# The first batch reordered and mixed at full width, with q and k loaded in two pieces instead of four, in an attention and Fourier-mix kernel

## The chip, the cores and the metric

The kernel runs on one core of a Trainium2 chip. The metric is the device time of one execution in microseconds (us). TensorE multiplies matrices, VectorE, ScalarE and GpSimd work on elements, and SyncE issues most of the transfers. In the profile they are called PE, DVE, ACT, POOL and SP; PEld is TensorE's loading of weights.

## What is computed

Eight batches, 576 positions, 8 heads of 64 channels. Attention is done in chunks of 64 positions; its output, seen as 512 channels per position, goes through a Fourier mix, a normalization and a feed-forward block:

```python
# attention, per batch and head, 9 chunks of 64 positions
scores = (q_c @ k_c.T) / 8
attn   = softmax(scores)
x      = attn @ v_c                       # [8, 576, 512] once the heads are side by side
# Fourier mix and feed-forward
mixed  = real(fft(fft(x, axis=1), axis=2))
u      = x + mixed
un     = (u - mean(u)) / sqrt(var(u) + 1e-6)
out    = u + relu(un @ w_ch1) @ w_ch2     # w_ch1 [512, 2048], w_ch2 [2048, 512]
```

The weights come in as 64-bit floats and are turned into 32-bit ones on the chip, on VectorE and ScalarE together ("rounding").

## The kernel before

All work is laid out by hand in one order. A batch has four tiles of 128 positions: `LO` tiles hold positions from the front, `HI` tiles their mirror images from the back. Each two batches share a tile `RE` with the two middle chunks. That makes 36 tiles; 9 of them belong to the first two batches (`first[2]` is 9). The Fourier sums use the mirror symmetry: a pair `LO[i]`, `HI[i]` is first *folded* (sums and differences), then multiplied by cosine and sine tables along the positions (`z`), then along the channels (`mix`).

From the third batch on, q and k aren't transposed on TensorE but in 32 x 32 blocks on VectorE. For this each of q and k is loaded in runs of 224 elements that overlap (the same positions twice, the second time shifted by 32 channels), so that the transposed blocks of one head fill 64 partitions:

```python
    def load(n):                                   # tiles n >= first[2]
                (b0, c0), (b1, c1) = chunks(n)
                parts = [(0, 32, b0, min(c0, c1))] if b0 == b1 else [(0, 16, b0, c0), (16, 16, b1, c1)]
                for g in range(4):
                    e, x0 = g // 2, g % 2 * 32
                    for r0, rows, b, c in parts:
                        from_ = src[b, e:H:2, c * CH:c * CH + 4 * rows, :].rearrange("j (p t) d -> p j (t d)", t=4)
                        eng.dma_start(out=t[32 * g + r0:32 * g + r0 + rows, :, 0:4 * D - 32],
                                      in_=from_[:, :, x0:x0 + 4 * D - 32])
    def att_S(n):                                  # scores of one tile: 16 products, 64 x 64 x 64
        for j in range(NJ):
            for e in range(2):
                for c in range(2):
                    r0, t0 = e * D, c * CH
                    nc.tensor.matmul(out=sc[t0:t0 + CH, e, j * CH:(j + 1) * CH],
                                     lhsT=a[r0:r0 + D, 2 * j + c, 0:CH], rhs=b[r0:r0 + D, 2 * j + c, 0:CH],
                                     start=True, stop=True)
        ...                                        # DVE: mx (maximum), ex (difference); ACT: exp
```

The first batch has nothing to hide behind, and runs ahead of all else: its attention, its folds, its mix, its normalization. `keep_warm` issues products whose result nobody reads.

```python
    def shift_early(i):                            # one row of each LO tile moves to the next tile
        if i == 0:
            nc.gpsimd.tensor_copy(...)             # three rows
        else:
            nc.scalar.copy(...)                    # three rows
    def fold(b, i):
        eng = nc.vector if b < 2 and (b, i) != (0, NM) else nc.gpsimd
        ...                                        # sum, two, two, pm, pm
    def fourier(b):
        for pair in range(2):                      # z: products of the folded tiles with the position tables
            ...
        def mixed(i):                              # half of the channels: 129 + 128 + 256 + 128 columns
            ...
            nc.scalar.copy(y[:, 0:HM + 1], mix[:, 0:HM + 1])
            nc.scalar.copy(y[:, DM:DM + 1], mix[:, 0:1])
        def both(y, mix):                          # the mirrored half of the channels from the sine part
            nc.vector.tensor_tensor(out=y[:, DM - 1:HM:-1], in0=y[:, 1:HM], in1=mix[:, HM + 1:DM], op=ALU.subtract)
            nc.vector.tensor_tensor(out=y[:, 1:HM], in0=y[:, 1:HM], in1=mix[:, HM + 1:DM], op=ALU.add)
        ...
        if b == 0:
            y, g = [mixed(i) for i in range(NM)], groups[0]
            for i in range(NM):
                ...                                # both, added, means, normed (un), turned (pt, unT), per tile
    ...
        for step, _ in enumerate(fourier(0)):
            for _ in range((2, 1, 0)[step]):
                round_next()                       # one 128 x 512 piece of a weight: 5 DVE and 3 ACT operations
```

After that TensorE runs the feed-forward block group by group: `up_first` and `down_plain` for the first batch, later forms (`up_halves`, `down_halves`) that save products with sums of weight blocks kept in HBM. `keep2` makes those sums of the second weight on VectorE, `keep1` those of the first on GpSimd. The attention and the mix of the next batch are laid in between, step by step (`t` counts the steps; the first group has 32, `begin[1]` is 32):

```python
                for _ in range(2 if n_w <= len(pieces) else 3):
                    if n_w > N_LAST + 2 and n_conv < 5 or n_w > len(pieces):
                        n_conv += 1
                        next(conv2, None)          # one operation of keep2
                if t == begin[1] - 1:
                    for _ in conv2:
                        pass
                if begin[1] <= t < begin[1] + KF // 2:
                    for _ in range(3):
                        next(conv1, None)          # one operation of keep1
```

Of the kernel before, what the change touches and what calls it, by code (L numbers as in the profile page):

```python
# [16 lines left out]
def kernel(  # L17
# [94 lines left out]

    LO, HI, RE = "lo", "hi", "rest"
    tiles, first = [], []
    for b in range(B):
        first.append(len(tiles))
        if b % 2 == 0:
            tiles.append((RE, b, 0))
        tiles += [(what, b, i) for what in (LO, HI) for i in range(NM)]
# [41 lines left out]
    dims = [start[:, d0 + o:d0 + o + n_] for o, n_ in ((0, HM + 1), (HM + 1, HM - 1), (2 * HM, HM + 1), (3 * HM + 1, HM - 1))]  # L161
# [3 lines left out]
    def load(n):  # L165

        for src, dst, nm, eng in ((q, qs, "q", nc.sync), (k, ks, "k", nc.scalar if n == 0 else nc.sync)):  # L170
            if n < first[1]:
                i = 2 * n + (nm == "k")
                t = start[:, (4 + i) * DM:(5 + i) * DM].rearrange("p (j r d) -> p j (r d)", r=2, d=D)
            else:
                t = one_p.tile([128, NJ, 4 * D], FP32, tag=nm, name=nm)
            if n >= first[2]:
                (b0, c0), (b1, c1) = chunks(n)
                parts = [(0, 32, b0, min(c0, c1))] if b0 == b1 else [(0, 16, b0, c0), (16, 16, b1, c1)]
                for g in range(4):
                    e, x0 = g // 2, g % 2 * 32  # L180
                    for r0, rows, b, c in parts:
                        from_ = src[b, e:H:2, c * CH:c * CH + 4 * rows, :].rearrange("j (p t) d -> p j (t d)", t=4)
                        eng.dma_start(
                            out=t[32 * g + r0:32 * g + r0 + rows, :, 0:4 * D - 32],
                            in_=from_[:, :, x0:x0 + 4 * D - 32],
                        )
                dst[n] = t
                continue
            t = t.rearrange("p j (r d) -> p (j r) d", d=D)[:, 0:H]
            (b0, c0), (b1, c1) = chunks(n)  # L190
            if b0 == b1 and c1 == c0 + 1:
                parts = [(0, 128, b0, c0)]
            else:
                parts = [(0, CH, b0, c0), (CH, CH, b1, c1)]
            for p0, np_, b, c in parts:
                eng.dma_start(
                    out=t[p0:p0 + np_], in_=src[b, :, c * CH:c * CH + np_, :].rearrange("h p d -> p h d")
                )
            dst[n] = t
# [15 lines left out]
    def load_tables():  # L215

        t = start[:, 0:(NM + 1) * 2 * NQ].rearrange("p (i r f) -> p i r f", i=NM + 1, r=2)  # L220
        for c in range(2 * NM):
            (i, r0), (j, p0) = divmod(c * CH, 128), divmod((NC - 1 - c) * CH, 128)
            nc.gpsimd.dma_start(out=t[r0:r0 + CH, i], in_=seq_tab[p0:p0 + CH, j])
        for r0 in (0, CH):
            nc.gpsimd.dma_start(out=t[r0:r0 + 1, NM], in_=seq_tab[0:1, 0])
            nc.gpsimd.dma_start(out=t[r0 + 1:r0 + CH, NM], in_=seq_tab[1:CH, NM])

    def load_dim_tables():
        nc.gpsimd.dma_start(out=dims[0], in_=dim_tab[:, 0, 0:HM + 1])
        nc.gpsimd.dma_start(out=dims[1], in_=dim_tab[:, 2, 1:HM])  # L230
        nc.gpsimd.dma_start(out=dims[2][0:1], in_=dim_tab[0:1, 1, 0:HM + 1])
        nc.gpsimd.dma_start(out=dims[3][0:1], in_=dim_tab[0:1, 3, 1:HM])

    def turn_tables():
# [5 lines left out]
        nc.gpsimd.tensor_copy(a[:, :, NL + 1:NQ], b[:, :, NL + 1:NQ])  # L240
        nc.gpsimd.memset(cx[:, 0:HQ + 1], 0.0)
        nc.gpsimd.tensor_copy(ce, dims[0][:, ::2])
        nc.gpsimd.tensor_copy(co, dims[0][:, 1::2])
        nc.gpsimd.tensor_copy(so, dims[1][:, ::2])
        nc.gpsimd.tensor_copy(so[0:1], dims[3][0:1, ::2])
        nc.gpsimd.tensor_copy(cx[:, HQ + 1:HM], dims[1][:, 1::2])
        nc.gpsimd.memset(cx[0:1, HQ + 1:HM], 0.0)
        nc.gpsimd.tensor_copy(cx[0:1, 0:HQ + 1], dims[2][0:1, ::2])
# [58 lines left out]
    def att_T(n):  # L307
# [4 lines left out]
        if n >= first[2]:  # L312
            for src, dst, nm in ((qs, qT, "qT"), (ks, kT, "kT")):
                a = src.pop(n).rearrange("p j (t b d) -> p j t b d", t=4, b=2)[:, :, :, 0]
# [3 lines left out]
                if kind(n) == HI:  # L318
                    to = to[:, :, ::-1]
                nc.vector.transpose(out=to.rearrange("p j c (r t) -> p j t c r", t=4), in_=a)  # L320
                if low:
                    nc.gpsimd.tensor_copy(t[:, :, :, 0:1], t[:, :, :, CH:CH + 1])
                dst[n] = t.rearrange("p j c t -> p (j c) t")
# [8 lines left out]
        if low and n == at[LO, 0, 1]:  # L332
            nc.scalar.copy(t[:, :, 0:1], t[:, :, CH:CH + 1])
        elif low:
            nc.gpsimd.tensor_copy(t[:, :, 0:1], t[:, :, CH:CH + 1])
# [5 lines left out]
        kT[n] = t.rearrange("p j (c t) -> p (j c) t", c=2)  # L341
# [3 lines left out]
    def att_S(n):  # L345
        a, b = qT.pop(n), kT.pop(n)
        sc = ps_a.tile([128, 2, 512], FP32, tag="att", name="sc")
        for j in range(NJ):
            for e in range(2):
                for c in range(2):  # L350
# [4 lines left out]
                        rhs=b[r0:r0 + D, 2 * j + c, 0:CH],  # L355
# [28 lines left out]
    def att_V(n):  # L384
# [35 lines left out]
        if kind(n) == HI:  # L420
            nc.gpsimd.tensor_copy(x[:, 0:1], x[:, DM:DM + 1])
# [3 lines left out]
    def shift_early(i):  # L425

        lows = [xt(at[LO, 0, j])[:, 0:DM] for j in range(NM)]
        rest = xt(rests[0])[0:1, 0:DM]
        if i == 0:
            nc.gpsimd.tensor_copy(first_rest[CH:CH + 1, 0:DM], rest)  # L430
            nc.gpsimd.tensor_copy(rest, lows[0][0:1])
            nc.gpsimd.tensor_copy(lows[0][0:1], lows[0][CH:CH + 1])
        else:
            nc.scalar.copy(lows[0][CH:CH + 1], lows[1][0:1])
            nc.scalar.copy(lows[1][0:1], lows[1][CH:CH + 1])
            nc.scalar.copy(lows[1][CH:CH + 1], first_rest[CH:CH + 1, 0:DM])
# [15 lines left out]
    def fold(b, i):  # L452

        eng = nc.vector if b < 2 and (b, i) != (0, NM) else nc.gpsimd
        two = one_p.tile([128, 2 * (HM + 1)], FP32, tag="two", name="two")
        if i < NM:
# [3 lines left out]
            nc.gpsimd.memset(s[:, DM:DM + 1], 0.0)  # L460
# [27 lines left out]
    def attention_early():  # L488
# [3 lines left out]
        def ready(n):  # L492
            for i in range(NM):
                if n == at[LO, 0, i]:
                    shift_early(i)
                if n == at[HI, 0, i]:
                    fold(0, i)
            if n == at[LO, 0, 0]:
                fold(0, NM)
            if n + 3 > hi:  # L500
# [55 lines left out]

    def fourier(b):
# [11 lines left out]
        for pair in range(2):  # L569
            if b == 0 and pair == 1:  # L570
                z = early_xp[0]
            else:
                z = [ps_t.tile([128, 512], FP32, tag="pt", name="z") for _ in range(2)]
# [59 lines left out]
        def added(y, n):  # L633
            x, w = xt(n), DM + (kind(n) == HI)
            eng = nc.gpsimd if kind(n) == HI and b > 0 else nc.vector
            eng.tensor_tensor(out=x[:, 0:w], in0=y[:, 0:w], in1=x[:, 0:w], op=ALU.add)  # L636

        def means(ns):
            st = sm_p.tile([128, 2, 2], FP32, tag="st", bufs=6 + NP, name="st")
            rstd = sm_p.tile([128, 2], FP32, tag="rstd", bufs=6 + NP, name="rstd")  # L640
            for j, n in enumerate(ns):
                bst = sm_p.tile([128, 6], FP32, tag="bst", name="bst")
                nc.vector.bn_stats(bst, xt(n)[:, 0:DM])  # L643
                nc.vector.bn_aggr(st[:, j], bst)  # L644
                sts[n] = st[:, j, 0:1], rstd[:, j:j + 1]
            g = slice(0, len(ns))
            nc.scalar.activation(out=rstd[:, g], in_=st[:, g, 1], func=ACTF.Ln, bias=eps)
            nc.scalar.activation(out=rstd[:, g], in_=rstd[:, g], func=ACTF.Exp, scale=-0.5)

        if b == 0:  # L650
            y, g = [mixed(i) for i in range(NM)], groups[0]
            def turned_(s):
                keep_warm(2)
                turned(0, s)

            keep_warm(4)
            for i in range(NM):
                y_ = both(*y[i])
                if i > 0:
                    normed(0, 1)  # L660
                    turned_(1)
                added(y_, g[2 * i])
                means(g[2 * i:2 * i + 1])
                added(y_, g[2 * i + 1])
                normed(0, 2 * i)
                means(g[2 * i + 1:2 * i + 2])
                turned_(2 * i)
            normed(0, 3)
            turned_(3)
            yield  # L670
            return
        for i in ((NM,) if h == 1 else ()) + tuple(range(NM)):
# [5 lines left out]
            yield  # L678

# [305 lines left out]
    with tc.manual_schedule():  # L985
# [6 lines left out]
        for n in range(3):  # L992
            load(n)
            load_v(n)
        for n in range(3, first[1]):
            load(n)
        for n in range(3, first[1]):
            load_v(n)
# [18 lines left out]
        for step, _ in enumerate(attention_early()):  # L1017
            if step == 0:
                load_tables()
                load_dim_tables()  # L1020
# [3 lines left out]
        keep_warm(5)  # L1024
        for step, _ in enumerate(fourier(0)):
            for _ in range((2, 1, 0)[step]):
# [29 lines left out]
        for g in range(NG):  # L1056
            for _ in mlp(g):
# [17 lines left out]
                for _ in range(2 if n_w <= len(pieces) else 3):  # L1075
# [3 lines left out]
                if t == begin[1] - 1:  # L1079
                    for _ in conv2:  # L1080
                        pass
                if begin[1] <= t < begin[1] + KF // 2:
# [57 lines left out]
```

## Time and profile before

| | before |
|---|---|
| time, median of 3 runs | 1139.6 us (1138.49 to 1141.79) |
| span of the profiled run | 1140.0 us, mean granted TensorE clock 0.995 |
| first product of the feed-forward block | at 65.10 us |
| TensorE busy in the 65.10 us before it | 43.56 us |
| TensorE busy in the 1074.90 us after it | 1050.21 us |
| VectorE, ScalarE, GpSimd busy in the span | 599.2, 290.3, 274.3 us |
| HBM read and written | 166.96 MB, 24.12 MB |

A line of the timeline gives start, duration, engine, line of the kernel, operation, what is written from what, shape, and the number of records merged into it; in brackets stands the idle time of the engine before it and what ended that. TensorE takes each 32-bit product in two passes, so a product has two records; a transposition has one. A line of the waits gives the total in us, how many times, and the longest.

### The profile page before, as it was taken

The numbers are of one execution on the slowest core, as the hardware profiler recorded it, in microseconds if no ns is written. First come the engines' busy times: TensorE is split into PE (matmuls) and PEld (weight loads), VectorE is DVE, ScalarE is ACT, GpSimd is POOL, SyncE is SP. The second block draws the span as 40 slices with busy tenths as digits, with TensorE's granted clock in tenths as the row PEclk, the third lists the DMA queues.
The fourth block names the chain that finished last, engine by engine and source line by source line (L and its number), as shares of the span: only waits on it lengthen the run. The fifth ranks groups of instructions, "written<-read, shape, count | busy, mean of one in ns | idle before, by whom it ended". The sixth has DMA issues, their size and how long they took to land. (4 is left out here: it accounts for less than half of the span.)

```text
span 1140.0 us, 18688 instructions
## 1 busy us (share of the span) xinstructions
PE 1093.8 (96%) x7040; PEld 846.3 (74%) x7040; DVE 599.2 (53%) x1241; ACT 290.3 (25%) x711; POOL 274.3 (24%) x406
## 2 busy tenths in 40 slices
PE   5789998999999999999999999899999999999998
PEld 4544444445888888778888888788888888888887
DVE  4699978524356445563556365654555434423521
ACT  3577652121202221222113211321032202201210
POOL 4100101336400531043305140063015400130140
PEclk9999998999999999999999999999999999999999
DMA  9737652787556725773466546662664246446332
GB/s 172 221 96 210 177 175 72 225 262 234 211 168 188 234 96 181 230 198 118 165 209 173 176 140 203 179 206 111 187 203 125 84 161 197 128 145 214 94 108 77
DMA packets 150123, 192.47 MB, mean 169 GB/s; under 512 B 68820, under 2 KB 106713, under 8 KB 142865
## 3 DMA queue, kind: packets, MB, share of 16 engines
q1 hardware_dynamic: 147184, 189.57, 54.7%
q0 software_dynamic: 704, 1.17, 0.5%
q8 instruction: 56, 0.92, 0.3%
q10 hardware_dynamic: 2144, 0.52, 0.3%
q14 instruction: 35, 0.28, 0.1%
HBM read 166.96 MB, written 24.12 MB: 168 GB/s over the span
## 5 line engine op out<-in xcount | busy, mean ns | idle before, releaser
L791 POOL TENSOR_TENSOR h<-h 128x256 f32<-128x256 f32 x64 | 55.4, 871 | 415.6 <-PE pb L885 303.3
L932 PE MATMUL pa<-wb,h 128*128 128x256 f32 x512 | 116.1, 381 | 0.0
L932 PE MATMUL pb<-wb,h 128*128 128x256 f32 x512 | 115.0, 381 | 0.0
L885 PE MATMUL pb<-unT,wa 128*128 128x256 f32 x448 | 106.7, 381 | 4.4 <-DVE wa L894 4.4
L885 PE MATMUL pb<-wa 128*128 128x256 f32 x448 | 107.1, 382 | 0.8 <-DMA wa<-s 0.6
L885 PE MATMUL pa<-unT,wa 128*128 128x256 f32 x448 | 107.8, 383 | 0.0
L932 PEld LDWEIGHTS pa<-wb,h 128*128 128x128 f32 x512 | 95.8, 190 | 14.6 <-issue 1.6
L932 PEld LDWEIGHTS pb<-wb,h 128*128 128x128 f32 x512 | 95.8, 190 | 12.9
L885 PEld LDWEIGHTS pb<-unT,wa 128*128 128x128 f32 x448 | 84.2, 190 | 18.9 <-DVE wa L894 7.6
L885 PEld LDWEIGHTS pb<-wa 128*128 128x128 f32 x448 | 83.5, 190 | 13.7 <-DVE wa L892 1.2
L885 PEld LDWEIGHTS pa<-unT,wa 128*128 128x128 f32 x448 | 83.2, 190 | 11.6
L900 ACT ACTIVATE h<-pa 128x256 f32<-128x256 f32 x56 | 21.5, 384 | 176.2 <-PE pa L885 143.2
L839 PE MATMUL dn<-wb,h 128*128 128x512 f32 x128 | 60.6, 623 | 1.9 <-ACT h L809 1.9
L801 PE MATMUL up<-unT,wa 128*128 128x512 f32 x128 | 58.0, 599 | 1.7 <-ACT h L809 0.9
L892 DVE TENSOR_TENSOR wa<-pa,wa 128x256 f32<-128x256 f32 x56 | 23.8, 425 | 66.5 <-PE pa L885 62.9
L932 PE MATMUL pa<-wb,yall 128*128 128x256 f32 x256 | 58.2, 382 | 0.0
L885 PE MATMUL pa<-wa 128*128 128x256 f32 x224 | 54.0, 384 | 3.8 <-ACT wa L890 3.8
L818 PE MATMUL up<-unT,wa 128*128 128x512 f32 x128 | 57.5, 598 | 0.0
L932 PE MATMUL pb<-wb,yall 128*128 128x256 f32 x256 | 57.1, 380 | 0.0
L932 PE MATMUL pb<-wb 128*128 128x256 f32 x256 | 56.6, 379 | 0.0
L932 PEld LDWEIGHTS pb<-wb 128*128 128x128 f32 x256 | 48.2, 190 | 6.3
L636 POOL TENSOR_TENSOR xall<-y,xall 128x513 f32<-128x513 f32 x14 | 21.3, 1522 | 131.1 <-DVE y L630 131.1
(211 smaller groups left out, 1698.5 us busy)
## 6 DMA issues: line engine op xcount, KB each, us to landing
wb<-s SPq DMA_DIRECT2D x56, 1024.0 KB
wa<-s SPq DMA_DIRECT2D x196, 256.0 KB
xall<-in_moe_w_ch_dram SPq DMA_DIRECT2D x22, 512.0 KB
q<-in_q_dram SPq DMA_DIRECT2D x96, 112.0 KB
k<-in_k_dram SPq DMA_DIRECT2D x96, 112.0 KB
v<-in_v_dram SPq DMA_DIRECT2D x132, 64.0 KB
yall<-in_moe_w_ch_dram SPq DMA_DIRECT2D x10, 512.0 KB
s<-wb SPq DMA_DIRECT2D x20, 256.0 KB
```

Source lines behind the costliest of these rows:

```text
L636: eng.tensor_tensor(out=x[:, 0:w], in0=y[:, 0:w], in1=x[:, 0:w], op=ALU.add)
L791: nc.gpsimd.tensor_tensor(out=h1[:, m, hi], in0=h1[:, m, lo], in1=h1[:, m, hi], op=ALU.subtract)
L801: nc.tensor.matmul(out=up, lhsT=w1[:, kk, m * 128:(m + 1) * 128], rhs=unT[:, kk], start=(kk == 0), stop=(kk == KD - 1),)
L818: nc.tensor.matmul(out=up, lhsT=w1[:, kk, m * 128:(m + 1) * 128], rhs=unT[:, kk], start=(kk == 0), stop=(kk == KD - 1),)
L839: nc.tensor.matmul(out=dn, lhsT=h1[:, m, s * 128:(s + 1) * 128], rhs=w2[:, m, :], start=(m == 0), stop=(m == KF - 1),)
L885: nc.tensor.matmul(out=dst, lhsT=w[:, kk, r], rhs=rhs[o][:, kk], start=(o in (0, 2) and kk == 0), stop=(kk == 1), skip_group_check=True,)
L892: nc.vector.tensor_tensor(out=b, in0=dst, in1=a, op=ALU.add)
L900: nc.scalar.activation(out=h1[:, m, lo], in_=dst, func=ACTF.Relu)
L932: nc.tensor.matmul(out=dst, lhsT=lhs[:, m], rhs=w[:, m], start=(o in (0, 2) and m == 0), stop=(m == HF - 1), skip_group_check=True,)
```

## The change

It has three parts, and isn't a step on top of the kernel before: the way in which q and k are loaded from the third batch on is exchanged for another, and two other things are changed.

- **q and k from the third batch on.** They are loaded as runs of 128 elements, each element once, in four transfers per tile and tensor (before: four, eight for `RE`). After the transposition the 64 channels of a head lie as two halves of 32 on the same partitions, so a score is the sum of two products of depth 32: 32 products per tile in place of 16.
- **The first batch.** Its tiles come in the order `RE, LO1, HI1, LO0, HI0`; q and k of later tiles are loaded ahead of v of earlier ones; all tables are loaded from SyncE after them. The pair 1 is folded by GpSimd while the attention of the pair 0 runs, the three rows that ScalarE moved are moved by GpSimd, `z` is done in the order pair 1, middle, pair 0, and the mix multiplies by the tables of all 512 channels, so that the copies `y` and the operations `both` fall away.
- **The sums of the second weight** (`keep2`). Once the weights are rounded, one operation is issued per step in place of three, three only for the last steps; what is left is issued at `begin[1] + 1`, and `keep1` starts two steps later.

```diff
-        tiles += [(what, b, i) for what in (LO, HI) for i in range(NM)]
+        tiles += [(LO, 0, 1), (HI, 0, 1), (LO, 0, 0), (HI, 0, 0)] if b == 0 else [
+            (what, b, i) for what in (LO, HI) for i in range(NM)
+        ]
 ...
             if n >= first[2]:
-                (b0, c0), (b1, c1) = chunks(n)
-                parts = [(0, 32, b0, min(c0, c1))] if b0 == b1 else [(0, 16, b0, c0), (16, 16, b1, c1)]
-                for g in range(4):
-                    ...
+                for i, (b, c) in enumerate(chunks(n)):
+                    for e in range(2):
+                        r0 = i * CH + e * 32
                         eng.dma_start(
-                            out=t[32 * g + r0:32 * g + r0 + rows, :, 0:4 * D - 32],
-                            in_=from_[:, :, x0:x0 + 4 * D - 32],
+                            out=t[r0:r0 + 32].rearrange("p (j t) d -> p j (t d)", t=2),
+                            in_=src[b, e:H:2, c * CH:(c + 1) * CH, :].rearrange("j (p t) d -> p j (t d)", t=2),
                         )
 ...
-            nc.gpsimd.dma_start(out=t[r0:r0 + CH, i], in_=seq_tab[p0:p0 + CH, j])
+            nc.sync.dma_start(out=t[r0:r0 + CH, i], in_=seq_tab[p0:p0 + CH, j])
 ...
-        nc.gpsimd.dma_start(out=dims[0], in_=dim_tab[:, 0, 0:HM + 1])
-        nc.gpsimd.dma_start(out=dims[1], in_=dim_tab[:, 2, 1:HM])
-        ...
+        nc.sync.dma_start(out=cos_d, in_=dim_tab[:, 0, :])
+        nc.sync.dma_start(out=sin_d[1:128], in_=dim_tab[1:128, 2, :])
+            nc.sync.dma_start(out=sin_d[0:1, 0::2], in_=dim_tab[0:1, 1, 0::2])
+            nc.sync.dma_start(out=sin_d[0:1, 1::2], in_=dim_tab[0:1, 3, 1::2])
 ...
     def att_S(n):
+        for j in range(NJ if n >= first[2] else 0):
+            for c in range(2):
+                for h in range(2):
+                    for e in range(2):
+                        r0, t0 = c * CH + e * 32, c * CH
+                        nc.tensor.matmul(
+                            out=sc[t0:t0 + CH, e, j * CH:(j + 1) * CH],
+                            lhsT=a[r0:r0 + 32, j, h, 0:CH],
+                            rhs=b[r0:r0 + 32, j, h, 0:CH],
+                            start=(h == 0),
+                            stop=(h == 1),
+                        )
 ...
     def fold(b, i):
-        eng = nc.vector if b < 2 and (b, i) != (0, NM) else nc.gpsimd
+        eng = nc.vector if (b, i) == (0, 0) or b == 1 else nc.gpsimd
 ...
+    def fourier_early():
+        order = (1, NM, 0)
+        for i in order:
+            ...                                     # z of the four tables, then the middle channel
+        for T in range(4):                          # zf: half of the copies on DVE, half on ACT
+            ...
+        yield
+        for i in range(NM):
+            for T, tab in ((0, cos_d), (1, cos_d), (3, sin_d), (2, sin_d)):
+                nc.tensor.matmul(
+                    out=early_xp[0][i][:, T % 2::2], lhsT=zf[:, T, 128 * i:128 * (i + 1)], rhs=tab[:, T % 2::2],
+                    start=(T == 0), stop=(T == 2), skip_group_check=True,
+                )
+        keep_warm(4)
+        yield
+        for i in range(NM):                         # added straight from the product; means, un, turned as before
+            ...
 ...
-        for n in range(3):
-            load(n)
-            load_v(n)
-        for n in range(3, first[1]):
-            load(n)
-        for n in range(3, first[1]):
-            load_v(n)
+        for what, n in (
+            (load, 0), (load_v, 0), (load, 1), (load, 2), (load_v, 1), (load, 3), (load_v, 2), (load, 4),
+        ):
+            what(n)
+        load_tables()
+        load_v(3)
+        load_v(4)
+        load_dim_tables()
 ...
-        for step, _ in enumerate(fourier(0)):
-            for _ in range((2, 1, 0)[step]):
+        for step, _ in enumerate(fourier_early()):
+            if step == 0:
+                turn_dim_tables()
+            for _ in range((2, 0, 1)[step]):
                 round_next()
 ...
-                for _ in range(2 if n_w <= len(pieces) else 3):
+                for _ in range(2 if n_w <= len(pieces) else 1 if t < begin[1] - 2 else 3):
 ...
-                if t == begin[1] - 1:
+                if t == begin[1] + 1:
                     for _ in conv2:
                         pass
-                if begin[1] <= t < begin[1] + KF // 2:
+                if begin[1] + 2 <= t < begin[1] + 2 + KF // 2:
```

## Prediction, made before the changed kernel was run

> **What bounds the kernel now.** The page comes first: TensorE is busy for nearly all of the span.
>
> ```profile
> span 1140.0 us, 18688 instructions
> PE 1093.8 (96%) x7040; PEld 846.3 (74%) x7040; DVE 599.2 (53%) x1241; ACT 290.3 (25%) x711; POOL 274.3 (24%) x406
> ```
>
> A busy share is an average, so I cut the span where the work changes (columns: busy us and records of PE, PEld, DVE, ACT, POOL; granted clock; DMA share; GB/s).
>
> ```profile
> 0.00:65.10 65.10, 43.56 (x517) 31.02 (x517) 38.01 (x89) 27.89 (x69) 17.26 (x49) 1.00 0.79 172
> 65.10:180.00 114.90, 111.93 (x588) 55.42 (x589) 100.71 (x202) 75.52 (x143) 4.49 (x12) 0.99 0.59 163
> 180.00:215.00 35.00, 29.37 (x170) 14.74 (x169) 27.51 (x48) 4.34 (x11) 11.89 (x12) 0.90 0.61 196
> 215.00:1140.00 925.00, 908.91 (x5769) 745.13 (x5767) 432.97 (x905) 182.54 (x489) 240.66 (x334) 1.00 0.54 168
> ```
>
> To be seen: up to 65.10 us TensorE waits for the first batch. From 215 us on it is busy in 908.91 of 925 us, so a product added there is paid in full. Between 180 and 215 us it idles and its clock is down. The waits of TensorE after 65 us name the cause:
>
> ```profile
> PE pt L303 <- DVE un L696: 7.4, 7, 5.6
> PE dn L839 <- ACT h L809: 1.9, 1, 1.9
> ```
>
> One wait of 5.6 us, for the normalized tile `un` of the second group. So there are three places to read: the start, that wait, and the cost of a score tile.
>
> **What the skill says.** The Trainium skill, "TensorEngine Tiling (Array Packing)", section Tiling Modes, has small tiles of the array working independently, and a drain where the mode changes; its Gotcha 1 says that different row tiles can't use one PSUM bank at once. The timeline agrees on the first two:
>
> ```profile
> 337.47 3.62 PE L932 MATMUL pb<-wb,h 128*128 128x256 f32 x16
> 341.02 0.69 PE L352 MATMUL sc<-kT,qT 64*64 64x64 f32 x32
> 341.64 1.99 PE L885 MATMUL pa<-unT,wa 128*128 128x256 f32 x8
> ```
>
> 32 records of 64 columns take 0.69 us with the 0.22 us that the last one lasts; one after another they would need far more. Four 64 x 64 tiles work side by side: eight rounds in 0.69 - 0.22 = 0.47 us, 59 ns each. On the bank no run here shows more: both kernels give `e` its own bank, but in the changed one rows 0-31 and 64-95 share a bank on different output partitions. The skill's "TensorE: Matmul & The Clock Gate", Part 1, has the clock halved after some 3.4 us without work; the trace agrees below. "DMA: Bandwidth & Descriptors", section Why a DMA increments its semaphore by 16 and not by 1, says that a transfer of 127 partitions goes to a single DMA engine; no transfer before has that shape. "GPSIMD Engine Reference", section 3, puts GpSimd at about half VectorE's speed for such sums; the groups agree, 1295 against 692 ns:
>
> ```profile
> L461 POOL TENSOR_TENSOR sum<-xall 128x512 f32<-128x512 f32 x12 | 15.5, 1295 | 3.8 <-DMA xall<-first 3.3
> L461 DVE TENSOR_TENSOR sum<-xall 128x512 f32<-128x512 f32 x4 | 2.8, 692 | 0.8 <-POOL sum L460 0.6
> ```
>
> **Part 1, q and k: slower.** A score tile gets 32 products for 16, so 64 records. They lie on four tiles of 32 rows x 64 columns, two per column half. If all four still work side by side, there are 16 rounds in place of 8: 8 x 59 ns = 0.47 us more per tile. 36 - 9 = 27 tiles are concerned (the block transpositions on VectorE are x27 in the groups). 27 x 0.47 = 12.7 us. Nothing lies beside it: it is TensorE's own time in the stage that TensorE bounds. The order of issue (two halves of one pair of heads, then of the other chunk) could keep only two tiles busy; then it is 24 more rounds, 1.4 us per tile, 38 us in all. I choose four. The transfers shrink from 112 to 64 KB each, 27 x 2 x (448 - 256) KB = 10 MB of 192 less; TensorE waits only 0.6 us for transfers after 65 us, so I count nothing. The transpositions (1.10 us) keep their number and size.
>
> **Part 2, the first batch: faster, by little.** The end of it now:
>
> ```profile
> 50.67 0.69 DVE L293 TENSOR_TENSOR wa<-wa,power 128x512 f32<-128x512 f32 x1
> 53.33 0.42 DVE L629 TENSOR_TENSOR y<-y,mix 128x255 f32<-128x255 f32 x1 [1.97 <-ACT y L625]
> 63.16 0.55 DVE L696 TENSOR_SCALAR un<-xall,st,rstd 128x512 f32<-128x512 f32 x1 [0.60 <-ACT rstd L648]
> ```
>
> ```profile
> 65.10 10.57 PE L801 MATMUL up<-unT,wa 128*128 128x512 f32 x24 [0.67 <-ACT unT L709]
> ```
>
> From the first `both` to the last `un` VectorE needs 53.33 to 63.7, 10.4 us; the transposition and its copy make it 65.1. Step by step for the changed kernel:
>
> - Attention: score tiles follow each other by 4.45 us where nothing else waits (15.45, 19.90); the next two came after 5.76 and 6.57 us, because k landed late (waits of 2.0 and 1.1 us) and ScalarE moved three rows (1.84 us). With the new loads and GpSimd for the rows the last score comes at about 28.8 instead of 32.2, its output at 34.7 instead of 39.7.
> - Folds: GpSimd's chain is pair 1 from 27.2 (4.6 us by its rows' means), the position tables (2.3), three rows (1.9), the middle (3.7): 40 us. VectorE's one fold (2.6) starts with the moved rows, at 36.3, and is done at 38.9. `z` of the middle waits for 40; with 1.2 us for it, 1.0 of keep-warm and 2.4 for the last pair, `z` ends near 45 against 47.7 now.
> - Rounding: the two pieces laid in there occupy VectorE and ScalarE (0.34 x 4 us, a wait for ScalarE's three operations, 1.9 us) until about 50, as they do until 51.4 now. The sine table `sin_d[1:128]` may go over one DMA engine; 127 rows of 2 KB at the 19 GB/s that one engine's sixteenth of 304 GB/s (30 to 40 us) gives are 14 us, and pieces queued behind it land near 48, which puts the end of rounding at 52.
> - Normalization: without `both` (4 x 0.45 us) and the wait for `y`, 9.0 us, then 1.4 as now. 50 or 52 + 10.4: the feed-forward starts at 60.5 to 62.5.
>
> So 2.6 to 4.6 us are won. But the third piece is now rounded after the normalization, not before: VectorE enters the feed-forward some 2.6 us later against it (five operations, 2.6 us per piece). The first four steps ask for two pieces each, and `h` already waited there for ScalarE (0.93 us). I take 1 us back. Net -2.5 us.
>
> **Part 3, the sums: faster.**
>
> ```profile
> 182.75 7.13 PE L839 MATMUL dn<-wb,h 128*128 128x512 f32 x16
> 195.51 1.08 PE L303 MATMUL pt<-ident,un 128*128 128x128 f32 x4 [5.63 <-DVE un L696]
> 197.24 4.74 PE L839 MATMUL dn<-wb,h 128*128 128x512 f32 x8
> ```
>
> VectorE reaches that `un` late because sums stand before it in its queue. In the changed order five fewer do: two before the second mix, one before the maximum, two before `un`; at 0.6 us each 3.0 us. TensorE's wait falls from 5.6 to about 2.6 us. After it, eight products took 4.74 us and not 3.6, and four transpositions 1.08 and not 0.60 (twice): the lowered clock costs 2 us more, and a wait below 3.4 us should be spared it. Together -5 us. The sums left over come when VectorE has room (it waits 2.7 to 6.4 us for scores from 217 us on). `keep1` starts two steps later, but there SyncE's queue, not GpSimd, set the time: the wait of `wb` for transfers (7.3 us, until 260.1) stays about as it is.
>
> **The sum.** +12.7 - 2.5 - 5 = +5.2 us: 1139.6 becomes about 1144.8.
>
> **Rivals.** (a) The scores run two tiles at a time, by order of issue or by the shared bank: +38 instead of +12.7, 1170 us. For it: the halves follow each other on the same rows. Against it: the first passes of four products start within 20 ns now, so TensorE looks well ahead. (b) The first batch wins its full 5 to 8 us, because the sine table is spread over the engines, rounding ends early and the backlog is absorbed: 1139 to 1141. For it: VectorE is idle for 2.2 us at 43.8 and 2.0 at 51.4 now. Against: 100.71 us of 114.90 are busy afterwards. (c) The late sums hold up VectorE or the queue between 215 and 280 us, and a wait appears there: +5 to +8, 1151. `xp` has one buffer, so a late VectorE stops TensorE. (d) One DMA engine's queue also blocks SyncE, and all weights come late: the first batch loses 3 us, 1149.
>
> **Range and chances.** The terms err apart from each other: scores +12 to +15 unless (a), start -7 to +2, sums -8 to +1. That gives 1137 to 1157 for eight in ten. 2% is 22.8 us: faster by that would need more than the start can give, slower by that needs (a).
>
> **What would show it.** The score groups of depth 32 with 64 records in about 1.16 us (0.47 more); a first `up` between 60 and 63 us; the wait for `un` below 3 us and no lowered clock after it; no new wait between 215 and 285. Wrong I am above all if a score tile costs more than 1.6 us, or if the first `up` comes before 58 us.

## The result and the profile after

| | before | after |
|---|---|---|
| time, median | 1139.7 us (4 runs, 1138.5 to 1141.8) | 1152.4 us (4 runs, 1151.0 to 1155.7) |
| ratio after / before | | 1.0114, 95% interval 1.0087 to 1.0141 |
| span of the profiled execution | 1140.0 us | 1151.5 us |
| TensorE busy | 1093.8 us | 1109.1 us |
| VectorE busy | 599.2 us | 579.8 us |
| HBM read | 166.96 MB | 156.60 MB |

The changed kernel is slower by 12.7 us. The time lies within the range that was predicted, but it is not made of the predicted parts. First the head of the page of the changed kernel:

```profile
span 1151.5 us, 20375 instructions
PE 1109.1 (96%) x7902; PEld 862.3 (75%) x7902; DVE 579.8 (50%) x1238; ACT 287.0 (25%) x700; POOL 274.9 (24%) x401
```

TensorE has 862 records more; 27 score tiles with 32 more each make 864, two are missing from the trace. VectorE, to which the change was not expected to give much, is busy 19 us less.

The span cut at the same clock times in both kernels (columns as in the prediction: busy us and records of PE, PEld, DVE, ACT, POOL; granted clock; DMA share; GB/s). Of the changed kernel:

```profile
180.00:208.00 28.00, 26.00 (x167) 13.55 (x166) 20.52 (x39) 4.34 (x11) 2.12 (x4) 0.94 0.37 113
215.00:290.00 75.00, 66.45 (x419) 33.96 (x418) 21.29 (x38) 13.05 (x27) 37.53 (x49) 0.95 0.74 231
```

And of the kernel before:

```profile
180.00:208.00 28.00, 22.37 (x121) 11.34 (x120) 24.20 (x43) 4.34 (x11) 5.04 (x6) 0.88 0.53 175
215.00:290.00 75.00, 74.31 (x421) 38.32 (x419) 27.08 (x46) 15.23 (x31) 31.52 (x45) 1.00 0.75 225
```

In the stage of the wait for `un` TensorE works 3.6 us more than before, which was intended. In the next stage, 215 to 290 us, it works 7.9 us less and at a lower clock. That stage was full before. So what was won at `un` comes back one group later, and more with it. The waits of TensorE from 62 us on name the places:

```profile
PE xp L407 <- issue: 5.9, 1, 5.9
PE pt L305 <- DVE un L763: 3.7, 7, 2.0
...
PE sc L353 <- DVE xall L426: 2.7, 1, 2.7
```

Two of them, 5.9 us at an `xp` and 2.7 us at a score tile, are not in the kernel before at all. The timeline of TensorE in the changed kernel (start, duration, then what it is; in brackets the idle time before):

```profile
62.58 5.85 PE L868 MATMUL up<-unT,wa 128*128 128x512 f32 x13 [0.68 <-ACT unT L776]
...
187.76 0.81 PE L305 MATMUL pt<-ident,un 128*128 128x128 f32 x4 [2.00 <-DVE un L763]
...
189.22 4.73 PE L906 MATMUL dn<-wb,h 128*128 128x512 f32 x8
...
230.62 1.21 PE L353 MATMUL sc<-kT,qT 32*64 32x64 f32 x64 [2.69 <-DVE xall L426]
...
269.21 1.13 PE L407 MATMUL xp<-v,pT 64*64 64x64 f32 x32 [5.86 <-issue]
270.27 12.11 PE L885 MATMUL up<-unT,wa 128*128 128x512 f32 x24
```

To be seen: the first `up` at 62.58 us, as predicted. The wait for `un` is down from 5.63 to 2.00 us, also as predicted, but the eight products after it still take 4.73 us, so the lowered clock is not spared. A score tile of 64 records takes 1.21 us in place of 0.69. Then the two new waits; behind the second one 24 products take 12.11 us in place of 10.57.

Both new waits are waits for VectorE, and VectorE itself waits for transfers. The timeline of VectorE in the changed kernel:

```profile
229.87 0.69 DVE L426 TENSOR_TENSOR xall<-xp,rd 128x512 f32<-128x512 f32 x1 [14.46 <-DMA s<-xall]
...
265.64 0.42 DVE L856 TENSOR_TENSOR wb<-h 128x256 f32<-128x256 f32 x1 [16.02 <-DMA s<-wb]
```

The first is the output of the attention. Its place in `xall` holds the last sums of the second weight until they are written out. (Why that took until 229.8 us is told below, with the stores.) The second is the first of the operations `operands`; its target is the space from which the last sums of the first weight (`keep1`) are written out. While VectorE stands there, the `xp` tile behind it in its queue is not read, and `xp` and `sc` share one buffer, so TensorE stops. In the kernel before, the first of these waits does not appear and the second ended at 260.13 us.

From 285 us on no new wait is left, and the lag behind the kernel before grows by 1.5 us in most stages of the second product and hardly at all in those of the first.

### The profile page after: what moved, and what is told of

It reads as the page before. It is cut to its first block, busy times and chain, and to the rows that moved or that the text cites. A ratio compares the mean times of both kernels' runs of the same rounds, so it can differ in the third digit from the quotient of the medians.

```text
span 1151.5 us, 20375 instructions
## 1 busy us (share of the span) xinstructions
PE 1109.1 (96%) x7902; PEld 862.3 (75%) x7902; DVE 579.8 (50%) x1238; ACT 287.0 (25%) x700; POOL 274.9 (24%) x401
## 3 DMA queue, kind: packets, MB, share of 16 engines
q8 instruction: 63, 1.03, 0.4%
HBM read 156.60 MB, written 24.12 MB: 157 GB/s over the span
## 5 line engine op out<-in xcount | busy, mean ns | idle before, releaser
L952 PEld LDWEIGHTS pb<-wa 128*128 128x128 f32 x448 | 83.5, 190 | 12.5 <-issue 1.2
L999 PEld LDWEIGHTS pa<-wb,yall 128*128 128x128 f32 x256 | 47.7, 190 | 6.9 <-issue 0.5
```

The lines of the kernel that those rows point to most:

```text
L952: nc.tensor.matmul(out=dst, lhsT=w[:, kk, r], rhs=rhs[o][:, kk], start=(o in (0, 2) and kk == 0), stop=(kk == 1), skip_group_check=True,)
L999: nc.tensor.matmul(out=dst, lhsT=lhs[:, m], rhs=w[:, m], start=(o in (0, 2) and m == 0), stop=(m == HF - 1), skip_group_check=True,)
```

## Experiments

A ratio is to the kernel before, run beside it on the same chip, with its 95% interval.

| run | what it is | median, us | ratio |
|---|---|---|---|
| qk_only | part 1 alone | 1148.6 | 1.0070 (1.0057 to 1.0083) |
| first_only | part 2 alone | 1138.1 | 0.9977 (0.9968 to 0.9986) |
| sums_only | part 3 alone | 1150.1 | 1.0085 (1.0070 to 1.0099) |
| both_on_time | all, `keep1` and the last sums when before | 1148.7 | 1.0069 (1.0056 to 1.0082) |
| spread_only | part 3 alone, with the same repair | 1145.4 | 1.0045 (1.0030 to 1.0061) |
| spread_late_ops | the same, `operands` of group 1 later | 1146.7 | 1.0047 (1.0028 to 1.0065) |
| best | first batch + spread_late_ops | 1143.2 | 1.0024 (1.0014 to 1.0034) |
| store_by_act | all, stores of group 0 from ScalarE | 1156.1 | 1.0139 (1.0124 to 1.0154) |
| qk_half_again | part 1, half of each transposition twice | 1155.9 | 1.0132 (1.0116 to 1.0147) |
| first_sine | first batch, sine table in two transfers | 1138.5 | 0.9983 (0.9975 to 0.9990) |
| first_T_early | first batch, transpositions earlier | 1137.1 | 0.9972 (0.9962 to 0.9981) |
| first_T_even | the same in two batches only | 1132.5 | 0.9927 (0.9907 to 0.9947) |

### The three parts, each alone

Each takes its hunks of the diff and leaves the rest as it was.

> Theory (the waits at 230 and 269 us of the changed kernel come from the sums, not from q and k): 27 score tiles x 0.51 us = 13.8 us more at most; some of it falls where TensorE waits for VectorE or ScalarE anyway (in the two-halves first product), so 8 to 12 us: 1148 to 1152 us, no new wait between 215 and 285 us. Rival (the longer score tiles push VectorE back and make those waits): the waits of 2.7 and 5.9 us are here too, 1157 us or more.

> Theory (the sums issued late hold up VectorE): the wait for un falls from 5.6 to 2 or 3 us (-3 to -5 us), and new waits of TensorE of 5 to 10 us in all appear between 215 and 285 us: 1141 to 1147 us. Rival (part three was right as predicted): -5 us and nothing new, 1134 to 1136 us.

> Theory: the first up begins near 62.6 us in place of 65.1 and this stays to the end: 1136.5 to 1138 us. Rival (the lead is taken back by waits for VectorE in the first two groups, since a piece of the weight is rounded later): the lead shrinks below 1 us before 215 us, 1139 to 1140 us.

Measured against their own runs of the kernel before: +8.1, +9.6 and -2.4 us. Part 1 has no new wait between 215 and 285 us: its theory holds, and the rival falls. Part 2 has its first `up` at 63.52 us, later than the theory had, and still 2.98 us of lead at 277 us; 1138.1 us is the edge of the theory's range, so it holds in kind. Some 1.6 us of the 2.98 come between 134 and 212 us and can't be put down to the change: behind the same wait of 1.90 us eight products take 3.70 us in this profile and 5.40 us, at a lowered clock, in that of the kernel before. Part 3 is slower by 9.6 us, more than even the theory had. Its waits of TensorE:

```profile
PE xp L395 <- issue: 6.5, 1, 6.5
PE pt L303 <- DVE un L696: 5.9, 10, 2.5
...
PE sc L352 <- DVE xall L414: 3.8, 1, 3.8
```

The wait for `un` does fall to 2.5 us, and the two waits in group 1 are those of the changed kernel. So the part meant to save 5 us costs 10, with q and k as they were. The three add up to +15.3 us, the whole change has +12.7. Its interval is 9.9 to 16.1 us, so the 2.6 us between them are not clear of noise.

### Are the two delays the cause, or the spreading?

```diff
-                if t == begin[1] + 1:
+                if t == begin[1] - 1:
                     for _ in conv2:
...
-                if begin[1] + 2 <= t < begin[1] + 2 + KF // 2:
+                if begin[1] <= t < begin[1] + KF // 2:
```

> The changed kernel with the sums left over issued at begin[1] - 1 and keep1 at begin[1], as in the kernel before; the spreading itself stays. Theory (the delay of these two makes the waits): the waits at 230 and 269 us go, 8 to 11 us: 1141 to 1145 us, and the wait for un stays near 2 us. Rival (the spreading or q and k make them): 1149 to 1153 us.

The wait at the score tile is gone and the one at `xp` is 2.9 us. Against its own runs of before it is +8.2 us where the changed kernel has +12.7: 4.5 us come back, half of what the theory said. So the delays are one part of the cause, and the spreading itself should be the other. That was then tried alone:

> The kernel before with the sums of the second weight spread as in the change, but flushed at begin[1] - 1 and keep1 at begin[1] as before. Theory (SyncE's queue in the first product of group 1 sets a time by the clock, so the 5 us won at un meet a floor near 260 us): the wait for un falls to 2 or 3 us, VectorE's wait for the transfers of wb still ends near 258 to 261 us, and a new wait of TensorE of 1 to 4 us appears there: 1136.5 to 1140 us. Rival (the queue has room, the waits came from the two delays alone): 1134 to 1136 us and no new wait.

This is +4.8 us, half of what part 3 costs, and slower than both theories had it. The wait for `un` is 2.5 us, as hoped, and then:

```profile
266.93 0.83 PE L395 MATMUL xp<-v,pT 64*64 64x64 f32 x32 [4.77 <-issue]
```

while VectorE in the same kernel shows

```profile
262.71 0.43 DVE L789 TENSOR_TENSOR wb<-h 128x256 f32<-128x256 f32 x1 [14.26 <-DMA s<-wb]
```

The transfers of `wb` end at 262.71 us in place of 260.13, although `keep1` is issued at the step of before. TensorE meanwhile would have been there 4.3 us earlier. The wait can be split in each run into these two: how much earlier TensorE comes to this `xp` (start less wait, before: 266.50 us), and how much later the `xall` operation ahead of it ends on VectorE (before: 264.28 us, so there are 2.22 us of slack).

| run | TensorE there earlier by | VectorE ready later by | sum less 2.22 | wait seen | last `s<-wb` issued at | GB/s from 200 to 215 us |
|---|---|---|---|---|---|---|
| before | 0 | 0 | none | none | 259.03 | 314 |
| first_only | 2.98 | -3.35 | none | none | 255.76 | 287 |
| both_on_time | 7.06 | -2.07 | 2.8 | 2.88 | 257.64 | 249 |
| spread_only | 4.34 | 2.54 | 4.7 | 4.77 | 261.57 | 221 |
| after | 3.15 | 4.82 | 5.8 | 5.86 | 264.55 | 176 |
| sums_only | -3.13 | 11.79 | 6.4 | 6.55 | 270.88 | 225 |

The fourth column must come near the fifth, since TensorE starts as soon as VectorE is ready; the table tells the shares. Two things are read from it. Only 2.22 us of any lead at `un` can be kept as long as the transfers end when they did. And wherever the sums are spread, the stretch from 200 to 215 us moves 176 to 249 GB/s in place of 314 (first_only, without spreading, 287; in `after` and both_on_time the smaller q and k are a part of it): the transfers that it doesn't carry are still to be done afterwards. first_only is earlier in both columns by about the same amount, and so keeps its lead.

### Does VectorE's place in line make the floor, or do the transfers?

`operands` of group 1 from `m` = 12 on, two per step, so that VectorE comes to the wait when it should be over:

```diff
-            if g >= first_of[2] and m > HF:
-                operands(h1, m - HF - 1)
+            if g >= first_of[2] and m >= HF + 4:
+                for i in range(2 * (m - HF - 4), min(2 * (m - HF - 4) + 2, HF - 1)):
+                    operands(h1, i)
```

> The same, with the operands of group 1 computed from m = 12 on, two per step, in place of from m = 9 on, one per step: VectorE then reaches the wait for the transfers of wb some 10 us later, when they are done. Theory (the floor acts through VectorE's queue and the single xp buffer): the new wait goes, 1133.5 to 1136.5 us. Rival (other transfers behind them in SyncE's queue hold TensorE): no faster than the kernel without this edit, 1137 to 1140 us.

> The new first batch, q and k as before, the sums spread but on time, the operands of group 1 late. Theory (the start's 2.4 us and the 5 us at un add up once nothing takes them back): 1131 to 1134.5 us. Rival (the lead meets the floor of SyncE's queue again): 1136 to 1138.5 us.

The wait at `xp` is down to 0.9 us, and nothing is won: 1.0047 against 1.0045. In its place TensorE's waits show

```profile
PE pa L933 <- DMA wb<-s: 2.8, 1, 2.8
PE z L564 <- POOL pm L477: 2.6, 1, 2.6
```

that is, the first slab of the second weight, and a fold that needs rows moved through SyncE's queue. Both stand behind the same transfers. "best", with the first batch's lead on top, runs into the same two (2.7 and 2.7 us): spreading, with the late operands, costs 5 us there too, 1143.2 against 1138.1 us of first_only. Its rival was right in kind and still too good. So it is not VectorE's order alone: with that wait gone, other transfers of the same row hold up group 1.

### Is it the order in SyncE's queue?

In the changed kernel the stores of group 0 stand in SyncE's queue from 211.75 to 219.33 us, ahead of the last sums. They were issued from ScalarE:

```diff
-                    store(n, o)
+                    store(n, o, nc.scalar)
```

> The changed kernel with the stores of groups 0 (and of the other plain down product, if any) issued from ScalarE in place of SyncE; nothing else moves, and the same bytes go out. Theory (it is the order in SyncE's queue: the last sums of the second weight stand behind these stores from 211.8 to 219.3 us, and all of keep1 behind them): VectorE's wait for the transfers of xall ends near 222 us in place of 229.9, the waits of TensorE near 230 and 269 us (2.7 and 5.9 us) shrink below 3 us together: 1143 to 1147 us. Rival (the DMA engines are the limit, not the queue's order): the waits shrink by less than 2 us, 1150 to 1153 us.

It is slower: 1156.1 us, waits of 3.6 and 6.8 us. The queue of SyncE has the stores no longer, but

```profile
205.54 12.06 SPq L837 DMA_DIRECT2D s<-yall  x3
```

three issues of sums now lie in 12.06 us, in the changed kernel in 2.47. The issues themselves take 0.41, 2.16 and 0.32 us; between the second and the third the queue waits for a store. Its waits from 195 to 240 us:

```profile
SPq L837 <- DMA out_dram<-o: 14.2, 2, 9.1
```

And ScalarE, which has to issue the stores, was stopped:

```profile
217.00 0.59 ACT L388 COPY pT<-pt 128x512 f32<-128x512 f32 x1 [18.74 <-DMA out_dram<-o]
```

The theory of the queue's order falls: a store holds up later transfers whichever engine issues it. What the two share is in the records of the transfers and their semaphores. In this program the transfers of SyncE and ScalarE carry eight semaphores in turn, and each waits before its issue until the last transfer on its own semaphore has landed. The third sum was issued at 217.27 us, when ScalarE's store of 206.65 us, on the same semaphore, had landed at 217.21. In the changed kernel the sum `s<-wb` issued at 226.51 us had waited in this way for the store of 213.98 us, which landed at 226.49.

Why the stores land so late: the Trainium skill, "DMA: Bandwidth & Descriptors", section Why a DMA increments its semaphore by 16 and not by 1, lets the number of DMA engines of a transfer follow from the size of its slowest dimension; the stores of `LO` tiles have 2 there (`c p d`), which would put each on two engines. The trace agrees: it records the landing of each engine's part, and such a store has two after its issue, at 226.48 and 226.49 us for the one of 213.98, where a transfer of 128 partitions has 16. Transfers behind it come late in two of their 16 parts. Of the sum `s<-xall` issued at 220.73 us in the changed kernel 14 parts had landed by 225.73 us and the last two at 229.77; it is this one that VectorE waited for until 229.8 us. In the kernel before, all sums of the second weight are issued by 209.63 us, ahead of the first store at 217.23. So for the first of the two new waits the way from the stores to VectorE is seen in the trace; whether splitting the stores would win the time wasn't tried.

### Where half of the scores' cost went

27 tiles at 0.51 us (from one score group's start to the next product 1.14 us, before 0.63) are 13.8 us, but part 1 alone costs 8.1. What else it changes is the transposition on VectorE. In the kernel before, q's row in the view of that line (min/median/max in ns, then the first and last start):

```profile
L320 DVE STREAM_TRANSPOSE qT<-q x27: 1087/1101/1124, 129.4 to 833.2; 128x512 f32<-128x512 f32 x27
```

After:

```profile
L320 DVE STREAM_TRANSPOSE qT<-q x27: 701/704/725, 127.1 to 844.1; 128x512 f32<-128x512 f32 x27
```

Same number, same size, 0.40 us less each (for k 1.085 and 0.670 us). In groups 3 and 5 they stand on VectorE ahead of the sum for which `pb` waits. These waits of the kernel before, in total, how many times, and the longest:

```profile
PE pb L885 <- DVE wa L894: 4.4, 5, 1.0
```

One of them on VectorE:

```profile
480.54 1.09 DVE L320 STREAM_TRANSPOSE qT<-q 128x512 f32<-128x512 f32 x1
481.48 1.06 DVE L320 STREAM_TRANSPOSE kT<-k 128x512 f32<-128x512 f32 x1
482.39 0.73 DVE L894 TENSOR_TENSOR wa<-pb,wa 128x256 f32<-128x256 f32 x2
```

with TensorE behind them:

```profile
482.85 1.99 PE L885 MATMUL pb<-unT,wa 128*128 128x256 f32 x8 [1.03 <-DVE wa L894]
```

and in qk_only:

```profile
484.65 1.99 PE L890 MATMUL pb<-unT,wa 128*128 128x256 f32 x8 [0.38 <-DVE wa L899]
```

To test it, half of each transposition was done a second time:

```diff
-                nc.vector.transpose(out=to.rearrange("p j b (t r) -> p j r b t", r=2), in_=a)
+                to = to.rearrange("p j b (t r) -> p j r b t", r=2)
+                nc.vector.transpose(out=to, in_=a)
+                nc.vector.transpose(out=to[:, 0:2], in_=a[:, 0:2])
```

> Part one alone, with half of each transposition of q and k done a second time (0.3 to 0.4 us more each on VectorE, about the 1.10 us of the kernel before). Theory (the 5 to 6 us of score time that do not appear in part one alone are paid back by the transpositions, which fell from 1.10 to 0.70 us and stand before the sum that pb waits for): the waits of pb for VectorE come back to about 1.0 us each, 4 to 5 us in all: 1152 to 1155 us. Rival (paid back elsewhere): 1148 to 1149.5 us, as part one alone.

The second halves took 0.446 us each, a little more than the 0.40 that had been saved. The four waits rose from 0.38 to 1.34 us, 3.84 us in all, and the time by 7.2 us, a little above the range. So the theory holds in kind. Of the 7.4 us between the two profiled spans the four waits make 3.84. Another 3.9 arise before the first product of group 1; 0.8 of these are there at the first `up` already, ahead of any transposition by blocks, so they aren't made by the edit. The rest, about 3 us, falls where VectorE is nearly full (in the kernel before busy for 100.71 of 114.90 us up to 180 us), and wasn't traced to a wait.

With this, part 1 adds up in its own profile. In the first two groups 3.0 us disappear (five tiles are 2.55 us, yet the second product of group 1 begins 0.41 us earlier than before): TensorE's wait for `h` at 132 us is 1.24 us in place of 1.90, the eight products after it take 3.70 us in place of 5.40 since no lowered clock follows, and the wait for `un` is 0.5 us shorter, 2.9 us together. After that 22 tiles are 11.2 us and the lag grows by 7.14: four waits of `pb` are 0.65 us shorter (2.6 us), one of 0.6 us for a slab and one of 0.19 us are gone. 11.2 - 3.4 = 7.8, near 7.14.

### The sine table

```diff
-        nc.sync.dma_start(out=sin_d[1:128], in_=dim_tab[1:128, 2, :])
+        nc.sync.dma_start(out=sin_d[1:113], in_=dim_tab[1:113, 2, :])
+        nc.sync.dma_start(out=sin_d[113:128], in_=dim_tab[113:128, 2, :])
```

> The new first batch alone, with the sine table in two transfers, 112 and 15 partitions, in place of one of 127. Theory (127 partitions go over one DMA engine, which delays the tables and the pieces of weight behind it): the tables are there before 42 us in place of 46, the first up begins 0.5 to 2 us earlier: 1136 to 1137.5 us. Rival (the tables wait in SyncE's queue, not on the engine; or rounding is bound otherwise): 1137.6 to 1139 us.

GpSimd's copy out of this table, first without and then with the edit:

```profile
48.20 0.29 POOL L252 COPY so<-start 128x128 f32<-128x128 f32 x1 [6.45 <-DMA start<-in_dim_tab_dram]
```

```profile
40.48 0.30 POOL L253 COPY so<-start 128x128 f32<-128x128 f32 x1
```

GpSimd's wait of 6.45 us is gone. The table in one transfer was issued at 30.73 us and landed at 47.70, with a single landing 16.97 us after the issue, that is, over one engine; in two it was issued by 29.60 us and landed by 35.01, with 16 and 15 landings. So the transfer of 127 partitions was slow, as the prediction had it, and 112 + 15 are not. Yet the two pieces of weight are rounded by 51.6 us in place of 53.0: VectorE now comes to them only at 47.15 us, behind the `zf` for which it waits 6.06 us. The time doesn't show the edit: 1138.5 us against 1138.1. The first `up` is 1.4 us earlier in this one profile (1.2 us of it come from an attention that ran earlier), and later waits of `pb` take that back. The slow transfer is real; its worth was nothing, as the rival had it.

### A version that beats both

The waits of `pb` are there in the kernel before as well, 1.03 us four times, and VectorE has 2.2 us of nothing to do just ahead of them. So the transpositions were issued directly behind the scores of the tile before:

```diff
             att_S(n)
+            if first[2] <= n + 1 < NT:
+                att_T(n + 1)
             yield
-            if n + 1 < NT and (b > 0 or n < hi):
+            if n + 1 < first[2] and (b > 0 or n < hi):
                 att_T(n + 1)
             yield
```

> The new first batch alone, with the transpositions of q and k issued directly behind the scores of the tile before, so that VectorE does them in the 2.2 us in which it waits for the second product of pa, not ahead of the sums that pb waits for. Theory (these transpositions are what pb waits for): the waits of pb for VectorE, 4.7 us, fall below 1 us: 1133 to 1135 us. Rival (something else in VectorE's queue takes their place, or q lands too late): 1137 to 1139 us.

1137.1 us: the rival. The waits are gone in groups 3 and 5, but 1.8 us appear in groups 2 and 4, in which the attention stands one step otherwise and the old place had been the free one; and the wait for `un` grew from 5.6 to 7.5 us. So only `b` = 4 and 6 were changed (`early = b in (4, 6)`):

> The new first batch alone, with the transpositions of q and k behind the scores only in the attention of b = 4 and 6, the two batches whose scores stand ahead of the wait of pb. Theory (in the other batches the earlier transposition only moved the wait of 1.8 us to another tile, and in b = 1 it put 1.9 us on un): the four waits of 1.0 to 1.4 us go and no other comes: 4 us less than the new first batch alone, 1133 to 1135 us. Rival (something else takes their place): 1136.5 to 1139 us.

1132.5 us, ratio 0.9927 (0.9907 to 0.9947): this is faster than the kernel before by 8 us and than the changed kernel by 20. Of the waits of `pb` for VectorE one is left:

```profile
PE pt L310 <- DVE un L761: 9.2, 8, 5.6
...
PE pb L950 <- DVE wa L959: 0.2, 1, 0.2
```

The 5.6 us at `un` are still in it. They are the price of having the sums early.

## Why the prediction was right, and where it was wrong

The median of 1152.4 us lies in the range of 1137 to 1157, and the change is under 2% as forecast, but it is 7.6 us above the number, by errors of opposite sign. That the range held is in part luck: with part 3 as measured and part 1 as predicted, the sum would have been 1139.7 + 12.7 - 2.4 + 9.6 = 1159.6 us, outside of it.

- **Part 1, +12.7 predicted, +8.1 measured.** The four tiles do work side by side: 64 records take 1.21 us, and the rival of two tiles at a time (+38 us) is refuted. The cost per tile was well sized: 0.51 in place of 0.47 us. What failed is "Nothing lies beside it: it is TensorE's own time in the stage that TensorE bounds", together with "the transpositions (1.10 us) keep their number and size". They did, but took 0.70 us, and TensorE did wait for VectorE in that stage: 4.4 us for `pb` stood in the list of waits of the kernel before. "TensorE bounds the stage" was an average over tiles, some of which had a wait right after the score.
- **Part 2, -2.5 predicted, -2.4 measured.** The first `up` came at 62.58 us in the changed kernel and at 63.52 alone, for 60.5 to 62.5. The slow sine table was real: 17.0 us from issue to landing for an estimate of 14. The wait for `h` at 79 us grew only to 1.17 us, so the 1 us taken back for the backlog is not seen as such. Whether the net came out right for the reasons given stays open.
- **Part 3, -5 predicted, +9.6 measured.** The wait for `un` fell to 2.00 us ("from 5.6 to about 2.6"): right. Two steps failed. The first: "there SyncE's queue, not GpSimd, set the time: the wait of `wb` for transfers (7.3 us, until 260.1) stays about as it is". It moved to 265.64, and a second wait arose, for `xall` (2.7 us of TensorE), behind the stores of group 0. And had it stayed, the lead would still have been lost, since TensorE needed the result only 2.22 us later than it had it; that slack wasn't looked up. A wait of 7.3 us on VectorE was read as harmless because TensorE didn't wait there, where the question was how far from waiting it was. The second: "a wait below 3.4 us should be spared it". 2.00 us were enough for the lowered clock, and the trace of the kernel before had shown it already, behind a wait of 1.90 us (the line is below).
- **The rivals.** (c) named the place, 215 to 280 us, the cause "the late sums hold up VectorE or the queue", and the way, `xp` with its one buffer; its 1151 us is within 1.5 us of the result. It was given as a rival, against a sum that took the gain at `un` for kept. (d) did not occur: the start was not late.
- **The signs.** The score groups and the first `up` came as named; "no lowered clock after it" and "no new wait between 215 and 285" both failed, and these two pointed at once to part 3.

In the kernel before, eight products that otherwise take 3.6 to 3.7 us:

```profile
134.25 5.40 PE L839 MATMUL dn<-wb,h 128*128 128x512 f32 x8 [1.90 <-ACT h L809]
```

## What to carry to other kernels

Before a wait is shortened, look one stage on: find what the engine meets next that is set by a clock of its own (here transfers that end at 260 us), and read how much slack it has there; a lead beyond that slack is given back. Work that looks as if it only fills an engine may be the feed of the transfers; putting it off leaves the DMA engines emptier now (176 GB/s in place of 314 from 200 to 215 us) and the transfers late afterwards. And a small operation on a half-busy engine can be worth its whole duration where it stands ahead of a sum that TensorE waits for: moving two transpositions by one step, in two batches, won about 5 us, twice what the one part of the change that won anything did.

## What the hardware showed that was not expected

- Transposing 128x512 by blocks took 1.09 us with one access pattern (every second group of 32 read, written four apart) and 0.69 us with another (all read, written two apart), in all 54 cases of each. Which of the two sides makes it wasn't tried.
- The lowered clock is half (products of 512 columns 0.85 us apart in place of 0.43) for 3.41 us or a multiple of it. It isn't set by the length of the idle time of TensorE before it alone. From the first `up` on, over all runs here, none of the idle times between 0.8 and 1.82 us was followed by it; of twelve between 1.88 and 2.00 us six were; all five between 2.2 and 2.51 us were; of six between 2.64 and 2.88 us four, and the wait of 2.69 us at the score tile of the changed kernel was not; all from 3.5 us on were. The Trainium skill, "TensorE: Matmul & The Clock Gate", Part 1, on which the prediction rested, has some 3.4 us; here less could be enough.
- A transfer over few of the DMA engines is slow, and holds up what comes behind it: 254 KB over one took 17.0 us, the first store of 256 KB over two 9.0 us in the changed kernel (211.75 to 220.71), the second, behind it, 12.5 us. Of a transfer of 16 parts issued at 220.73 us 14 had landed by 225.73 us, two only at 229.77.
- Rows 0-31 and 64-95 of the array write different partitions of one bank in the same stretch, and hardly any slowing is seen: the 16 rounds of a score tile took 1.21 - 0.22 = 0.99 us, 62 ns each, before 59 ns.
